# Last pair of row tiles: kept row tiles loaded through ScalarE's queue, last plain tile made by halves of columns in two banks

## The chip, the cores and the metric

The kernel runs on one core of a Trainium2 chip. The metric is the device time of one execution in microseconds (us), the median over runs. The engines are TensorE (PE; PEld is its loading of weights), VectorE (DVE), ScalarE (ACT), GpSimd (POOL) and SyncE (SP, which here only issues DMAs; SPq and ACTq are the queues of instructions that issue them).

## The reference

The output is `x + s * g` for a tensor x of 2048 rows and 448 columns. g is a gated network on the normalised rows; s is the real part of a Fourier transform over the columns and then over the rows, written as matrix products with given matrices:

```python
xn = _layernorm(x, axis=-1)
a = jnp.einsum("bsd,ed->bse", xn, dft_hid_re)
b = jnp.einsum("bsd,ed->bse", xn, dft_hid_im)
s = jnp.einsum("ts,bse->bte", dft_seq_re, a) - jnp.einsum("ts,bse->bte", dft_seq_im, b)
g = silu((gelu(xn @ w_gate) * (xn @ w_up)) @ w_down)
return x + s * g
```

## The kernel before

All matrix products are made from pairs: a number is split in a high part, in the matrix engine's 32-bit format, and a low part, the rest. A product is the sum of high by high, high by low and low by high. `split` makes the high part by a copy on ScalarE and the low part by a subtraction on VectorE.

The work goes in stages: normalised rows are turned and split; the gated network; the transform over columns (the tiles a and b); then the transform over rows, which fills the time from about 477 us on. This last stage alone is touched. It makes the 16 row tiles of the output (128 rows by 448 columns each) in eight pairs j = 0 to 7. A pair takes 16 steps, u0 to u15 in this text. In the steps u0 to u13 (`seven`) one of fourteen row tiles of the transformed input enters seven products of a scheme that needs seven products where eight would be usual; each product has a PSUM bank of its own, and takes a matmul of 448 columns and one of 224. In the last pair the steps u11 to u13 are ordered by product, so that products end one after another. The steps u14 and u15 (`plain`, called t0 and t1) are the two remaining input tiles, 12 matmuls for each of the two output tiles of the pair, in banks of their own (py0, py1). `gather` adds the seven products to the two output tiles c0 and c1 (in `cc`) on VectorE, after a first copy on ScalarE.

Each step needs coefficients: `load_c` loads them on SP's queue (ct and sums for a step of seven, cp for a plain one; in the end x), `sum_c` adds some of them on VectorE (L1208, L1209), and `prep_c` splits them (L149 on ScalarE, L150 on VectorE). In step m, `prep_c` splits for step m + 3, and then loads, into the buffer that came free, for step m + 8. So a late load holds a sum, then a split, and in the end PE.

Of the fourteen row tiles ten lie in SBUF for good. Four, called kept tiles here, share two places (`ts_u`, `ts_g`) and are read back from DRAM (`td`) in every pair, in eight pieces, one in each of u0 to u7 (L1386), on SP's queue. Each piece overwrites the part that PE read last, and waits for PE.

The order of every engine's instructions is that of the code, and an engine waits in order. DMAs of SP and ScalarE take eight semaphores in turn (DMAHW0 to 7): before one is issued, the DMA that used its semaphore last must have landed.

After the last step of the last pair, c1 is multiplied by its gate (`gx`), x is added, c0 gets py0, gate and x and is stored; then the last plain tile is multiplied by the gate, added to c1, and stored, by halves of columns (`sides`), one half on SP's and one on ScalarE's queue.

Of the kernel before, what the change touches and what calls it, by code (L numbers as in the profile page):

```python
# [8 lines left out]
F32 = mybir.dt.float32  # L9
# [4 lines left out]
P = 128  # L14
S = 2048
D = 448
# [28 lines left out]
KP = (10, 15)  # L45
# [14 lines left out]
def fnet_geglu(ctx: ExitStack, tc: tile.TileContext, xw, ca, ct, cp, et, wss, wd, out):  # L60
# [15 lines left out]
    nc = tc.nc  # L76
# [51 lines left out]
    def bank(i, name):  # L128
        return psum.tile([P, 512], F32, name=name, tag=f"b{i}")
# [425 lines left out]
    with tc.manual_schedule():  # L555
# [356 lines left out]
        h, l = [[v[:, n] for n in range(4)] for v in (xth[1], xtl[1])]  # L912
# [74 lines left out]
        for n, (p, f) in enumerate(blocks):  # L987
# [10 lines left out]
            if p == 0:  # L998
# [9 lines left out]
                if f in (8, 11):  # L1008

                    k = slice(0, 4, 3) if f == 8 else slice(1, 3)  # L1010
                    for i in range(2):
                        v, w = [u[:, i * 2048 :][:, :2048] for u in (sp, a_x[1].bitcast(F32))]
                        v, w = [u.rearrange("p (k d) -> p k d", k=4)[:, k] for u in (v, w)]
# [6 lines left out]
            elif f == 3:  # L1020

                late = then(late[0], t1_steps[7][2]), late[1]
                v = sb.tile([P, 8 * D], F32, name="gacc2", tag="u1")
# [3 lines left out]
                v = sb.tile([P, 4096], FR, name="w2", tag="u0")  # L1027
# [76 lines left out]
        TS, ab, behind = {}, {}, []  # L1104
# [108 lines left out]
        def prep_c(m):  # L1213

            if m >= len(units):
                return
            n = (4 if isinstance(units[m][1], str) else 7) * P
            h, l = [v[:, :n] for v in slot_at(m)]
            split(h, l, raw_at(m)[:, :n])
            c_hl[m] = h, l  # L1220
            n = nxt.get(m, m + 5)
            if n:
                load_c(n)
# [91 lines left out]

        sides = slice(0, HD), slice(HD, D)

        def plain(m, py):

            h, l = c_hl.pop(m)  # L1320
            for i, k in enumerate(KP):
                for r in range(2):
                    vh, vl = ab[k][r]
                    o = (2 * i + r) * P
                    a, b = h[:, o : o + P], l[:, o : o + P]
                    final = m == len(units) - 1 and i + r == 2
                    for e in sides if final else [slice(0, D)]:
                        for n, (w, v) in enumerate(((a, vh), (a, vl), (b, vh))):
                            nc.tensor.matmul(  # L1329
                                py[:, e], w, v[:, e], start=i + r + n == 0,  # L1330
                                stop=i + r == 2 and (final or n == 2), skip_group_check=m == len(units) - 1,
                            )

        def gather(ps):

# [29 lines left out]
        for m, (j, k) in enumerate(units):  # L1365
            u = m % UN
            end = j == NK // 2 - 1
            if u == 0:
                ps = {q: bank(banks[i], f"p{q}_{j}") for i, q in enumerate(PRODUCTS)}
            if k in KS:  # L1370
                if not end or u < NS - LAST:
                    seven(m, ps)
                elif u == NS - LAST:

                    seven(m, ps, last_steps)

                at = (0, 1, 2, 3, 4, 5, 6, 7) if j else range(LOAD_AT, LOAD_AT + 8)
                for i in range(8):
                    if u != at[i]:
                        continue  # L1380
                    i, h = divmod(i, 4)
                    TS[KX[(j + 1) % 2][i]] = TS[KX[j % 2][i]]
                    n = KX[(j + 1) % 2][i]
                    a, b = [v.rearrange("p (b d) -> p b d", d=D) for v in (TS[n], td[n])]
                    a, b = a[:, PARTS[h]], b[:, PARTS[h]]
                    nc.sync.dma_start(a.bitcast(F32), b)  # L1386
            else:
                py = bank(banks[7 if k == "t0" else 0], f"py{k[1]}_{j}")
                plain(m, py)
            if end and u in GX_END:  # L1390
                load_gx(j, GX_END.index(u))
            elif u == GX_AT[0]:
                load_gx(j, 0)
            elif u == GX_AT[1] and j:
                load_gx(j - 1, 1)

            if m:
                sum_c(m + 4)
            c0, c1 = cs[0][0], cs[1][0]
            if end and u == NS - LAST:  # L1400
                prep_c(m + 3)
                todo = gather(ps)
                todo.insert(2, lambda: prep_c(m + 4))
                todo.insert(7, lambda: nc.vector.tensor_add(c0, c0, cs[0][1]))
                todo.append(lambda: nc.vector.tensor_add(c1, c1, cs[1][1]))
                for f in todo:
                    f()
            elif end and u > NS - LAST:
                if u == NS:
                    py0 = py  # L1410
                if m < len(units) - 1:
                    continue
                x_ = [raw_at(m + 1 + t)[:, :D] for t in range(2)]
                y = raw_at(m + 3)[:, :D]
                nc.vector.tensor_mul(c1, c1, gx[1])
                nc.vector.tensor_add(c0, c0, py0[:, :D])
                nc.vector.tensor_add(c1, c1, x_[1])
                nc.vector.tensor_mul(c0, c0, gx[0])
                nc.vector.tensor_add(c0, c0, x_[0])
                nc.sync.dma_start(ov[:, NK - 2], c0)  # L1420
                for e in sides:
                    nc.vector.tensor_mul(y[:, e], gx[1][:, e], py[:, e])  # L1422
                for e, eng in zip(sides, (nc.sync, nc.scalar)):
                    nc.vector.tensor_add(c1[:, e], c1[:, e], y[:, e])
                    eng.dma_start(ov[:, NK - 1, e], c1[:, e])
            elif u == NS - 1 and not end:
                todo = gather(ps)
                for f in todo[:3]:
                    f()
                prep_c(m + 3)  # L1430
            elif u == NS and not end:
                for f in todo[3:]:
                    f()
                prep_c(m + 3)
                nc.scalar.activation(kept, py[:, :D], AF.Copy)
            elif u == NS + 1:
                prep_c(m + 3)
                spare = [lambda: nc.vector.tensor_add(c0, c0, kept)]
                spare += give(j, 0)
                spare.append(lambda py=py: nc.vector.tensor_add(c1, c1, py[:, :D]))  # L1440
                spare += give(j, 1)
                banks = banks[1:] + banks[:1]
            else:
                if m:
                    prep_c(m + 3)
                if m == 4:
                    sums14()
                if m == 6:
                    hid_split(14)()
                    load_c(14)  # L1450
                    load_c(15)
                if spare:
                    spare.pop(0)()
                if (u in STORE_AT or end and u == STORE_AT[1] - 1) and stores:
                    stores.pop(0)()
# [66 lines left out]
```

## Time and profile before

| | |
|---|---|
| Time, median of 3 runs | 767.68 us (767.65 to 768.83) |
| Profiled execution: time, span | 768.06 us, 766.3 us |
| PE busy | 760.3 us, 99% |
| PE weight loads busy | 686.6 us, 90% |
| VectorE busy | 637.2 us, 83% |
| ScalarE busy | 351.1 us, 46% |
| GpSimd busy | 120.1 us, 16% |
| Moved by DMA | 162.28 MB, 212 GB/s on average |

The span runs from the first to the last instruction of the profiled execution, 1.76 us less than its time. Busy times overlap between engines. In a timeline row stand start, duration, engine, line, operation and tiles (written <- read), their sizes, and in brackets how long the engine idled before it and what ended that. In a row of a DMA issue the last number is the time from its issue to its landing, in us.

### The profile page before, as it was taken

The page shows a single profiled execution, that of the slowest core. Times are in us where ns is not written, and L with a number is a line of the kernel's source. Part 1 is how long each engine was busy: PE and PEld are TensorE (multiplying, and loading weights), DVE is VectorE, ACT ScalarE, POOL GpSimd, SP SyncE. Part 2 cuts the span into 40 slices and gives each one's busy share as a digit, 9 for nine tenths or more (in the row PEclk, how much of TensorE's full clock was granted, in tenths as well). Part 3 has the DMA queues.
Part 4 walks back from the last instruction along what each step waited for, and adds up shares of the span by engine and source line. Part 5 has one row for each costly group of instructions (what it writes and reads, how often), then busy time and mean ns, then how long its engine had stood idle before and what let it go on. Part 6 is the DMA issues. An engine that isn't in the chain of part 4 may idle for free.

```text
span 766.3 us, 11497 instructions
## 1 busy us (share of the span) xinstructions
PE 760.3 (99%) x4044; PEld 686.6 (90%) x4044; DVE 637.2 (83%) x1088; ACT 351.1 (46%) x499; POOL 120.1 (16%) x162
## 2 busy tenths in 40 slices
PE   9999999999999999999999999999999999999997
PEld 8988888888888888888889999999999999999997
DVE  7987789889989988888975677988889797979786
ACT  5866443443434334343343755544444344444441
POOL 2002231423334223232200000000000000000000
PEclk9999999999999999999999999999999999999999
DMA  8077484849568563728742732869696969888794
GB/s 297 17 222 234 118 251 128 232 157 241 211 128 311 141 207 81 227 79 243 156 181 85 296 165 68 278 224 347 201 354 204 339 220 305 246 280 284 239 321 156
DMA packets 81034, 162.28 MB, mean 212 GB/s; under 512 B 8016, under 2 KB 62800, under 8 KB 79568
## 3 DMA queue, kind: packets, MB, share of 16 engines
q1 hardware_dynamic: 75648, 135.02, 51.6%
q0 software_dynamic: 5184, 26.41, 16.0%
q8 instruction: 32, 0.52, 0.3%
q14 instruction: 26, 0.21, 0.1%
q10 hardware_dynamic: 144, 0.11, 0.0%
HBM read 139.36 MB, written 51.25 MB: 249 GB/s over the span
## 4 chain that ended last, share of the span: by engine, by line
PE 98%; DMA 1%; POOL 0%; DVE 0%; SPq 0%; issue 0%; DVEq 0%
PE x L448 24%; PE p L1303 22%; PE po L422 18%; PE p L1306 10%; PE ab L1119 9%; PE py L1329 5%; PE x L460 4%; PE gu L371 3%; PE gu L596 2%; PE pt L206 1%; DMA raw<-xw 1%; POOL w L277 0%; SPq L156 0%; DVE w L272 0%; DVE f L1422 0%; SPq L260 0%
## 5 line engine op out<-in xcount | busy, mean ns | idle before, releaser
L422 PE MATMUL po<-wd,hs 128*128 128x448 f32 x672 | 146.4, 366 | 0.0
L422 PEld LDWEIGHTS po<-wd,hs 128*128 128x128 f32 x672 | 125.7, 188 | 12.4 <-DVE gacc L435 0.3
L448 PE MATMUL x<-xt,w 128*128 128x512 f32 x432 | 112.1, 390 | 0.0
L448 PEld LDWEIGHTS x<-xt,w 128*128 128x128 f32 x432 | 81.1, 188 | 15.9
L149 ACT ACTIVATE w<-raw 128x896 fp32r<-128x896 f32 (+1 forms) x59 | 53.6, 910 | 62.5 <-DVE raw L1209 21.9
L448 PE MATMUL x<-t,w 128*128 128x512 f32 x276 | 80.2, 390 | 0.0
L1119 PE MATMUL ab<-w,xt 128*128 128x448 f32 x256 | 68.1, 365 | 0.0
L435 DVE TENSOR_TENSOR gacc<-gacc,po 128x448 f32<-128x448 f32 x96 | 58.4, 613 | 5.4 <-PE po L422 5.0
L525 ACT ACTIVATE hs<-tmp 128x512 fp32r<-128x512 f32 x24 | 15.2, 633 | 103.5 <-DVE tmp L523 103.5
L448 PEld LDWEIGHTS x<-t,w 128*128 128x128 f32 x276 | 51.8, 188 | 9.9
L1303 PE MATMUL p<-xt,w 128*128 128x448 f32 x168 | 54.4, 374 | 0.0
L320 POOL TENSOR_TENSOR raw<-raw 128x256 f32<-128x256 f32 x23 | 19.5, 846 | 213.7 <-DMA raw<-wss 187.3
L1355 POOL DMA_DIRECT2D cc<-xw x14 | 12.3, 881 | 252.8 <-DVE raw L1208 96.2
L1119 PEld LDWEIGHTS ab<-w,xt 128*128 128x128 f32 x256 | 48.1, 188 | 3.8
L149 ACT ACTIVATE w<-f 128x896 fp32r<-128x896 f32 (+1 forms) x34 | 30.2, 888 | 40.7 <-DVE f L1209 13.5
L150 DVE TENSOR_TENSOR w<-raw,w 128x896 fp32r<-128x896 f32 (+1 forms) x40 | 41.7, 1045 | 2.0 <-ACT w L149 1.5
L1303 PE MATMUL p<-ts_g,w 128*128 128x448 f32 x112 | 36.4, 374 | 0.0
L1303 PE MATMUL p<-ts_u,ts_tmp 128*128 128x448 f32 x112 | 36.3, 374 | 0.0
L1303 PE MATMUL p<-hs,w 128*128 128x448 f32 x112 | 35.5, 374 | 0.0
L1119 PE MATMUL ab<-wd,xt 128*128 128x448 f32 x96 | 35.1, 365 | 0.0
L339 ACT ACTIVATE w<-raw 128x768 fp32r<-128x768 f32 x24 | 20.3, 845 | 30.3 <-POOL raw L326 30.1
L1303 PEld LDWEIGHTS p<-xt,w 128*128 128x128 f32 x168 | 31.5, 188 | 2.4
(281 smaller groups left out, 1825.8 us busy)
## 6 DMA issues: line engine op xcount, KB each, us to landing
sums<-ca SPq DMA_DIRECT2D x16, 896.0 KB, 8.7
sums<-ca POOLq DMA_DIRECT2D x16, 896.0 KB, 8.9
raw<-ct SPq DMA_DIRECT2D x69, 192.0 KB, 4.1
raw<-wss SPq DMA_DIRECT2D x24, 512.0 KB, 3.7
ts_u<-td SPq DMA_DIRECT2D x24, 448.0 KB, 5.8
ts_g<-td SPq DMA_DIRECT2D x24, 448.0 KB, 6.2
raw<-sums SPq DMA_DIRECT2D x69, 128.0 KB, 4.0
f<-ct SPq DMA_DIRECT2D x39, 192.0 KB, 4.6
```

What stands on the lines that cost most here:

```text
L149: nc.scalar.activation(h, src, AF.Copy)
L150: nc.vector.tensor_sub(l, src, h)
L339: nc.scalar.activation(h[:, :n], src[:, :n], AF.Copy)
L371: nc.tensor.matmul(ps[:, cols], a, xt[:, k, cols], start=n == 0, stop=n == len(mm) - 1)
L422: nc.tensor.matmul(po[:, :D], hs[:, a, kk * P : (kk + 1) * P], wdn[:, b, i], start=n == 0, stop=n == 5,)
L435: nc.vector.tensor_add(ga, ga, po[:, :D])
L448: nc.tensor.matmul(ps, a[i], b[j], start=first and n == 0, stop=n == 2, skip_group_check=True)
L460: nc.tensor.matmul(ps, a[0], x_, start=False, stop=True, skip_group_check=True)
L1119: nc.tensor.matmul(p[:, :D], a, b, start=n == 0, stop=n == len(mm) - 1)
L1303: nc.tensor.matmul(ps[q][:, :D], h, v, start=u % UN == 0, stop=False, skip_group_check=True)
L1306: nc.tensor.matmul(ps[q][:, :HD], l, v[:, :HD], start=False, stop=u % UN == NS - 1, skip_group_check=True,)
L1329: nc.tensor.matmul(py[:, e], w, v[:, e], start=i + r + n == 0, stop=i + r == 2 and (final or n == 2), skip_group_check=m == len(units) - 1,)
```

## The change

Four edits, all for the last pair of output tiles (`end`):

- the eight loads of kept tiles are issued on ScalarE's queue;
- in the last plain step (t1) the 12 matmuls are made for the left 224 columns first, in bank py1, and then for the right 224 in a second bank (py2), where before nine of them took all 448 columns and the last three came as two halves, in one bank;
- the last split (`prep_c(m + 4)` at u11) comes ahead of the copy and the sums of `gather`;
- at the end x is added to c1 before c0 gets py0, and each half of the last tile is multiplied and added before the next one's multiplication.

```diff
-        def plain(m, py):
+        def plain(m, *py):
 
             h, l = c_hl.pop(m)
-            for i, k in enumerate(KP):
-                for r in range(2):
-                    vh, vl = ab[k][r]
-                    o = (2 * i + r) * P
-                    a, b = h[:, o : o + P], l[:, o : o + P]
-                    final = m == len(units) - 1 and i + r == 2
-                    for e in sides if final else [slice(0, D)]:
-                        for n, (w, v) in enumerate(((a, vh), (a, vl), (b, vh))):
-                            nc.tensor.matmul(
-                                py[:, e], w, v[:, e], start=i + r + n == 0,
-                                stop=i + r == 2 and (final or n == 2), skip_group_check=m == len(units) - 1,
-                            )
+            for p, e in zip(py, sides) if len(py) > 1 else [(py[0], slice(0, D))]:
+                n = 0
+                for i, k in enumerate(KP):
+                    for r in range(2):
+                        vh, vl = ab[k][r]
+                        o = (2 * i + r) * P
+                        a, b = h[:, o : o + P], l[:, o : o + P]
+                        for w, v in ((a, vh), (a, vl), (b, vh)):
+                            nc.tensor.matmul(p[:, e], w, v[:, e], start=n == 0, stop=n == 11)
+                            n += 1
...
-                    nc.sync.dma_start(a.bitcast(F32), b)
+                    (nc.scalar if end else nc.sync).dma_start(a.bitcast(F32), b)
             else:
                 py = bank(banks[7 if k == "t0" else 0], f"py{k[1]}_{j}")
-                plain(m, py)
+                both_ = [py, bank(banks[1], "py2")] if m == len(units) - 1 else [py]
+                plain(m, *both_)
...
             if end and u == NS - LAST:
                 prep_c(m + 3)
+                prep_c(m + 4)
                 todo = gather(ps)
-                todo.insert(2, lambda: prep_c(m + 4))
-                todo.insert(7, lambda: nc.vector.tensor_add(c0, c0, cs[0][1]))
+                todo.insert(6, lambda: nc.vector.tensor_add(c0, c0, cs[0][1]))
...
                 nc.vector.tensor_mul(c1, c1, gx[1])
+                nc.vector.tensor_add(c1, c1, x_[1])
                 nc.vector.tensor_add(c0, c0, py0[:, :D])
-                nc.vector.tensor_add(c1, c1, x_[1])
                 nc.vector.tensor_mul(c0, c0, gx[0])
                 nc.vector.tensor_add(c0, c0, x_[0])
                 nc.sync.dma_start(ov[:, NK - 2], c0)
-                for e in sides:
-                    nc.vector.tensor_mul(y[:, e], gx[1][:, e], py[:, e])
-                for e, eng in zip(sides, (nc.sync, nc.scalar)):
+                for p, e, eng in zip(both_, sides, (nc.sync, nc.scalar)):
+                    nc.vector.tensor_mul(y[:, e], gx[1][:, e], p[:, e])
                     nc.vector.tensor_add(c1[:, e], c1[:, e], y[:, e])
                     eng.dma_start(ov[:, NK - 1, e], c1[:, e])
```

ScalarE, steps u4 to u7 of the last pair, with what each instruction waits for. L149 are the splits for the steps u7 to u10 (before, one more, for u11); `ts_g<-td` are pieces of a kept tile. Before:

```order
L149 ACTIVATE w<-f_3559 128x896 [waits DMAHW6_49,DVE_49,DMAHW7_49,PE_49,Activation_49]
L149 ACTIVATE ts_tmp<-f_3559 128x896 [waits DMAHW2_49,DVE_49,DMAHW3_49,PE_49,Activation_49]
L149 ACTIVATE w<-raw 128x896 [waits DMAHW5_49,DVE_49,DMAHW6_49,PE_49,Activation_49]
L149 ACTIVATE w<-raw 128x896 [waits DMAHW0_49,DVE_49,DMAHW1_49,PE_49,Activation_49]
L149 ACTIVATE w<-raw 128x896 [waits DMAHW3_49,DVE_49,DMAHW4_49,PE_49,Activation_49]
```

After:

```order
L1384 DMA ts_g_3513<-td_3364 128x2x448 [waits DMAHW3_49,DMASW5_49]
L149 ACTIVATE w<-f_3559 128x896 [waits DVE_49,DMAHW6_49,PE_49,Activation_49]
L1384 DMA ts_g_3513<-td_3364 128x896 [waits DMAHW6_49]
L149 ACTIVATE ts_tmp<-f_3559 128x896 [waits DVE_49,DMAHW4_49,PE_49,Activation_49]
L1384 DMA ts_g_3513<-td_3364 128x2x448 [waits DMAHW1_49]
L149 ACTIVATE w<-raw 128x896 [waits DVE_49,DMAHW7_49,PE_49,Activation_49]
L1384 DMA ts_g_3513<-td_3364 128x448 [waits DMAHW4_49]
L149 ACTIVATE w<-raw 128x896 [waits DVE_49,DMAHW2_49,PE_49,Activation_49]
```

A piece of a kept tile now stands ahead of each split, and waits for a semaphore of a load that SP issued earlier.

SP, steps u3 to u7: ct and sums load the coefficients of the steps u11, u12 and u13, cp those of u14 and u15. Before:

```order
L1201 DMA raw<-ct 128x384 [waits DMAHW3_49,DVE_49]
L1202 DMA raw<-sums_802 128x256 [waits DMAHW4_49]
L1386 DMA ts_g_3513<-td_3364 128x2x448 [waits DMAHW5_49,PE_49]
L1201 DMA f_3559<-ct 128x384 [waits DMAHW6_49,DVE_49]
L1202 DMA f_3559<-sums_802 128x256 [waits DMAHW7_49]
L1386 DMA ts_g_3513<-td_3364 128x896 [waits DMAHW0_49,PE_49]
L1201 DMA f_3559<-ct 128x384 [waits DMAHW1_49,DVE_49]
L1202 DMA f_3559<-sums_802 128x256 [waits DMAHW2_49]
L1386 DMA ts_g_3513<-td_3364 128x2x448 [waits DMAHW3_49,PE_49]
L1199 DMA raw<-cp 128x512 [waits DMAHW4_49,DVE_49]
```

After:

```order
L1201 DMA raw<-ct 128x384 [waits DMAHW4_49,DVE_49]
L1202 DMA raw<-sums_802 128x256 [waits DMAHW5_49]
L1201 DMA f_3559<-ct 128x384 [waits DMAHW7_49,DVE_49]
L1202 DMA f_3559<-sums_802 128x256 [waits DMAHW0_49]
L1201 DMA f_3559<-ct 128x384 [waits DMAHW3_49,DMAHW2_49,DVE_49]
L1202 DMA f_3559<-sums_802 128x256 [waits DMAHW3_49]
L1199 DMA raw<-cp 128x512 [waits DMAHW6_49,DMAHW5_49,DVE_49]
L1355 DMA out<-cc 128x448 [waits DMAHW6_49,DMASW2_49]
L1199 DMA raw<-cp 128x512 [waits DMAHW7_49,DMAHW1_49,DVE_49]
```

The pieces of kept tiles are gone from between the loads. The loads of u13 (third ct and sums) now wait for the semaphore (3) of the piece that ScalarE issues at u4, the last cp for that (1) of the piece at u6; the piece at u7 waits for the semaphore (4) of the first ct here.

VectorE, from the product of c1 and its gate to the end (f is a spare tile that takes the last plain tile times its gate). Before:

```order
L1415 TENSOR_TENSOR cc<-cc,ts_g_3513 128x448 [waits DMAHW4_49,DVE_49]
L1416 TENSOR_TENSOR cc<-cc,py_7_6709 128x448 [waits PE_49]
L1417 TENSOR_TENSOR cc<-cc,f_3559 128x448 [waits DMAHW2_49,DVE_49]
L1418 TENSOR_TENSOR cc<-cc,ts_g_3703 128x448 [waits DMAHW5_49,DVE_49]
L1419 TENSOR_TENSOR cc<-cc,raw 128x448 [waits DMAHW0_49,DVE_49]
L1422 TENSOR_TENSOR f_3559<-ts_g_3513,py_7_6723 128x224 [waits PE_49]
L1422 TENSOR_TENSOR f_3559<-ts_g_3513,py_7_6723 128x224
L1424 TENSOR_TENSOR cc<-cc,f_3559 128x224 [waits DVE_49] x2
```

After:

```order
L1414 TENSOR_TENSOR cc<-cc,ts_g_3513 128x448 [waits DMAHW4_49,DVE_49]
L1415 TENSOR_TENSOR cc<-cc,f_3559 128x448 [waits DMAHW2_49,DVE_49]
L1416 TENSOR_TENSOR cc<-cc,py_7_6709 128x448 [waits PE_49]
L1417 TENSOR_TENSOR cc<-cc,ts_g_3703 128x448 [waits DMAHW5_49,DVE_49]
L1418 TENSOR_TENSOR cc<-cc,raw 128x448 [waits DMAHW0_49,DVE_49]
L1421 TENSOR_TENSOR f_3559<-ts_g_3513,py_7_6723 128x224 [waits PE_49]
L1422 TENSOR_TENSOR cc<-cc,f_3559 128x224 [waits DVE_49]
L1421 TENSOR_TENSOR f_3559<-ts_g_3513,py_6724 128x224 [waits PE_49]
L1422 TENSOR_TENSOR cc<-cc,f_3559 128x224 [waits DVE_49]
```

Each half of the last plain tile now waits for its own bank, and each sum stands right behind its product.

## The prediction

> **What bounds the kernel now.** I read the page first (span, and the chain that ended last), then the busy time by stretches, the timeline of the last 15 us, and last each late DMA's issue and landing.
>
> ```profile
> span 766.3 us, 11497 instructions
> PE 98%; DMA 1%; POOL 0%; DVE 0%; SPq 0%; issue 0%; DVEq 0%
> ```
>
> The chain is the matrix engine's, 98% of the span. Does anything in the last pair of row tiles, the only place where the change acts, make it wait? The stretches (busy us of each engine, granted clock, DMA share, GB/s):
>
> ```profile
> 686.00:721.50 35.50, 35.50 (x222) 33.74 (x221) 29.79 (x58) 15.43 (x19) 1.75 (x2) 1.00 0.86 274
> 721.50:757.00 35.50, 35.50 (x222) 33.75 (x221) 31.01 (x58) 14.40 (x17) 1.77 (x2) 1.00 0.81 261
> 740.00:750.00 10.00, 10.00 (x66) 9.54 (x65) 6.94 (x14) 3.97 (x5) 0.90 (x1) 1.00 1.07 367
> ```
>
> No: PE is busy for all 35.50 us of the last pair (second row), as in the pair before it, at full clock. ScalarE is busy for 14.40 of them. The DMA engines are full between 740 and 750 (share 1.07, 367 GB/s). So earlier loads can buy nothing on PE; they can only keep a wait from appearing. What can shrink is what follows the last matmul:
>
> ```profile
> 756.78 1.39 PE L1329 MATMUL py<-ts_u,w 128*128 128x448 f32 x6
> 759.22 0.36 PE L1329 MATMUL py<-ts_u,ts_tmp 128*128 128x448 f32 x1
> 761.04 0.60 PE L1329 MATMUL py<-xt,ts_tmp 128*128 128x224 f32 x4
> 761.59 0.28 PE L1329 MATMUL py<-xt,ts_tmp 128*128 128x224 f32 x1
> 755.12 0.62 DVE L1343 TENSOR_TENSOR cc<-cc,p 128x448 f32<-128x448 f32 x1
> 758.69 0.63 DVE L1415 TENSOR_TENSOR cc<-cc,ts_g 128x448 f32<-128x448 f32 x1
> 759.42 0.62 DVE L1416 TENSOR_TENSOR cc<-cc,py 128x448 f32<-128x448 f32 x1
> 759.96 0.62 DVE L1417 TENSOR_TENSOR cc<-cc,f 128x448 f32<-128x448 f32 x1
> 760.50 0.62 DVE L1418 TENSOR_TENSOR cc<-cc,ts_g 128x448 f32<-128x448 f32 x1
> 761.14 0.62 DVE L1419 TENSOR_TENSOR cc<-cc,raw 128x448 f32<-128x448 f32 x1
> 761.90 0.69 DVE L1422 TENSOR_TENSOR f<-ts_g,py 128x224 f32<-128x224 f32 x2
> L1422 DVE TENSOR_TENSOR f<-ts_g,py x2: 380/384/388, 761.9 to 762.2; 128x224 f32<-128x224 f32 x2
> 762.51 0.69 DVE L1424 TENSOR_TENSOR cc<-cc,f 128x224 f32<-128x224 f32 x2
> 763.23 0.37 ACTq L1425 DMA_DIRECT2D out<-cc  x1
> out<-cc ACTq DMA_DIRECT2D x1, 112.0 KB, 1.7
> ```
>
> The last matmul ends at 761.59 + 0.28 = 761.87; VectorE (DVE) starts on the last plain tile at 761.90, ends at 763.20 with its four half-width steps, ScalarE's queue issues the last store at 763.23, it lands 1.7 us later (764.9), and 1.4 us close the span. The steps from 755.12 on come back to back, but for two short waits for PE: L1416 at 759.42 for the first plain tile, L1422 at 761.90 for the second.
>
> **The change, part by part.**
>
> *1. The last plain tile by halves.* It was 9 matmuls of 448 columns and 6 of 224; it becomes 24 of 224. Twelve of 448 take 759.22 - 756.78 = 2.44 us, 0.203 each; five steps of 224 take 761.59 - 761.04 = 0.55 us, 0.11 each. Two halves cost 0.22 where one whole cost 0.203, so nine split ones add 9 x 0.017 = 0.15 us. The first half ends at 759.22 + 11 x 0.11 + 0.28 = 760.71, the second at 759.22 + 23 x 0.11 + 0.28 = 762.03, 0.16 later than now. On the path only if DVE is ready by then.
>
> *2. DVE's last steps.* The add of x to the second tile moves ahead of the add that waits for the first plain tile. Two steps where the second needs the first lie 0.64 apart (760.50, 761.14), two that don't need each other 0.54 (759.42, 759.96). From 758.69: add x 759.33, add plain tile 759.87, multiply 760.51, add x 761.15; so the wait at 759.42 is exchanged for a dependence. Then the halves: multiply half 0 at 761.69 (done on PE since 760.71), add half 0, which needs the step just before: 0.384 + 0.03 = 0.41 later, 762.10; multiply half 1 at 0.30 after that (the distance that 0.69 for two of 0.384 leaves), 762.40, past PE's 762.03; add half 1 at 762.81, end 763.19. Now: 763.20. Half 0 starts 0.21 earlier and two dependences take it back: 0.0 us. Bounds: if PE alone set the end, 762.03 + 0.03 + 2 x 0.39 = 762.84, a gain of 0.36; if all four halves stood 0.41 apart from PE's later end, 762.06 + 3 x 0.41 + 0.38 = 763.67, a loss of 0.47. I take 0.0, because DVE's row of steps is unbroken and of the same count.
>
> *3. The gather.* The last split (tile ts_tmp) moves ahead of the copy of the first product on ScalarE, and its VectorE half ahead of the sums.
>
> ```profile
> 751.96 0.54 ACT L1338 ACTIVATE cc<-p 128x448 f32<-128x448 f32 x1 [0.99 <-PE p L1306]
> 753.80 0.68 DVE L150 TENSOR_TENSOR ts_tmp<-raw,ts_tmp 128x512 fp32r<-128x512 f32 x1
> 745.77 0.45 SPq L1199 DMA_DIRECT2D raw<-cp  x1
> raw<-cp SPq DMA_DIRECT2D x1, 256.0 KB, 6.2
> ```
>
> ScalarE idles 0.99 us before the copy, so a split fits if its data is there; but the load issued at 745.77 landed after 6.2 us, at 751.97. Landing there again, it would hold the copy back by the split's 0.6 us, to 752.6. The sums after it wait for PE again at 755.12 (L1343), and the 0.6 us of L150 are gone from between them, which absorbs it: four steps 0.54 apart from 753.2 reach L1343 at about 754.9. Cost 0; past a landing at about 752.2 each microsecond of lateness is one at the end.
>
> *4. The eight loads of kept tiles go to ScalarE's queue*, one in each of the steps u0 to u7 of the last pair. SP issues eight fewer. On ScalarE each costs an issue, 0.37 us by the store above, so 3.0 us, in steps where it is idle over half the time; behind each the split for three steps ahead is queued.
>
> ```profile
> 726.08 0.36 PE L1303 MATMUL p<-ts_u,ts_tmp 128*128 128x448 f32 x1
> 729.09 0.38 SPq L1386 DMA_DIRECT2D ts_u<-td  x1
> 733.22 0.96 ACT L149 ACTIVATE w<-raw 128x896 fp32r<-128x896 f32 x1 [1.36 <-DVE raw L1209]
> ```
>
> The first (now at 729.09) waits for the first two products of u0, which begins at 726.08; on ScalarE nothing else holds it, so it goes at about 727. A step takes 2.19 us (u10 begins at 748.00: 21.92 / 10). The fifth stands behind the split that ends at 734.18, so at about 735, the seventh two steps later, at about 739.4. Each load also waits until the DMA that last used its semaphore has landed. The worst off is the eighth: it waits for a load that SP issued at 736.16:
>
> ```profile
> 736.16 0.33 SPq L1201 DMA_DIRECT2D raw<-ct  x1
> raw<-ct SPq DMA_DIRECT2D x1, 192.0 KB, 6.7
> 741.57 0.95 ACT L149 ACTIVATE w<-raw 128x896 fp32r<-128x896 f32 x1 [1.20 <-PE p L1303]
> 743.86 1.08 DVE L150 TENSOR_TENSOR w<-raw,w 128x896 fp32r<-128x896 f32 x1
> 748.00 0.38 PE L1303 MATMUL p<-hs,w 128*128 128x448 f32 x1
> ```
>
> 736.16 + 6.7 = 742.9, plus the issue 743.2: the split of step u10 starts there instead of at 741.57, ends at 744.2, its VectorE half at 745.2 instead of 744.9, and PE comes to u10 at 748.00. It costs 0, since 2.8 us of lead remain.
>
> Where the lead is short is step u13:
>
> ```profile
> 740.28 0.33 SPq L1201 DMA_DIRECT2D f<-ct  x1
> f<-ct SPq DMA_DIRECT2D x1, 192.0 KB, 7.7
> 741.30 0.69 SPq L1202 DMA_DIRECT2D f<-sums  x1
> f<-sums SPq DMA_DIRECT2D x1, 128.0 KB, 7.1
> 748.48 0.29 DVE L1208 TENSOR_TENSOR f<-f 128x128 f32<-128x128 f32 x1 [1.43 <-DMA f<-sums]
> 750.25 1.09 DVE L150 TENSOR_TENSOR w<-f,w 128x896 fp32r<-128x896 f32 x1
> 751.66 0.26 PE L1306 MATMUL p<-ts_g,w 128*128 128x224 f32 x1
> ```
>
> Its two loads took 7.7 and 7.1 us; DVE waited 1.43 us for the second, and its low part is ready at 751.34, 0.32 us before PE uses it. With the kept tiles on another queue these loads no longer stand behind them. How fast then? At least as fast as this one, issued at 727.03 before the kept loads began; at worst as slow as now, after a later issue:
>
> ```profile
> raw<-sums SPq DMA_DIRECT2D x1, 128.0 KB, 2.4
> ```
>
> Between 2.4 and 7.1 I take about 5: the bytes stay and the engines are full, but the kept loads, issued from about 727 instead of 729, have their own line. Any value under 7.4 costs and gains nothing, since PE does not wait now.
>
> The Trainium skill ("DMA: Bandwidth & Descriptors", section "Issuing engines are not separate DMA queues") speaks against the load part: all issuers end on the same 16 DMA engines, and a second issuer saves only the issue time. The rows of 2.4 and 7.1 us show how much of a landing is waiting behind others, but no run here shows whether a second queue shortens it. By the rule the u13 loads land as late as now and the sum stays at 0, with 0.32 us to spare; by the rows it is 0 too, with some 2 us to spare. The rule bears only on the chance of a stall.
>
> **Sum.** 0.0 (halves and last steps) + 0 (gather) + 0 (loads) = 0.0 us on the profiled execution's 768.06 (766.3 and 1.76 around it). That execution is 0.38 above the median of 767.68; I put the sum on the median: 767.7 us.
>
> **Rivals.**
> *PE waits at step u13* (slower). The SP load of u13 now waits for a semaphore that the fifth kept load releases. If ScalarE issues that one at about 735 and it takes 7.1 us, as the u13 load does now, SP issues the second u13 load after 742.1, at about 742.5; at 7.1 us it lands at 749.6, 1.2 us later than now: 0.9 us of PE wait, 768.6. If the kept loads, on a line of their own, crowd the load to 8.5 us, it is 2.3 us, 770.0. It decides from a landing at 748.7. For it: full DMA engines, 0.32 us of lead. Against it: the two kept loads that stand among the loads just ahead of it are gone from its queue, and SP issues less.
> *The last load is late* (slower): its issue waits for the seventh kept load. From 739.4 and at 7.1 us that is 746.5, so the last load lands at 752.7, and the gather is 0.5 us past the point in part 3: 768.2. Against it: by then most loads are out.
> *The halves pay* (faster): DVE gets through its steps sooner and PE sets the end, 767.68 - 0.36 = 767.3. For it: half 0 is ready 1.3 us before half 1. Against it: DVE's steps show no gap to give up.
> *The second queue does nothing*: landings as now, 767.7 again.
>
> **How the numbers follow.** The forecast (no term reaches the end) 0.68; the second queue does nothing 0.08; the halves pay 0.08; PE waits at u13 0.12; the last load is late 0.04. A measurement of this kernel can tell about 0.2%, 1.5 us, from no change. Of the rivals only the longer stall at u13 passes that, half of its chance, 0.06; I keep 0.04 more for a stall at several steps and 0.03 for a gain that no row shows. So slower 0.10, same 0.87, faster 0.03. The range: below, the gain of 0.36 and as much again for the median's own spread, 767.1; above, the stall of 0.9 us and the spread to 768.9.
>
> **What would show it.** Right: PE without a gap to the end of the last tile, at about 762.0; L1421 on half 0 at about 761.7, the last store at 763.2; eight kept loads on ScalarE's queue from 727, issues near 0.37 us; the wait of 1.43 us before u13's sum shorter. Wrong: idle time on PE in the last six steps, a split on ScalarE over 2 us behind, the first product's copy later than 752.5, or landings on SP's queue over 7.4 us.

## The result and the profile after

| | before | after |
|---|---|---|
| Median (range), 22 runs each | 767.71 us (767.43 to 768.83) | 769.26 us (768.22 to 770.27) |
| Ratio after to before | | 1.0020, 95% interval 1.0014 to 1.0027 |
| Profiled execution: time, span | 768.06 us, 766.3 us | 768.22 us, 766.3 us |

The kernel became 1.55 us (0.2%) slower. The forecast was no change at 767.7 us, and 769.26 lies outside its range.

The profiled execution of the changed kernel is its quickest of 22. So a second execution of 769.42 us, "after, second profile", stands beside it; it stands for the median better. First the page of the first profile, then one stretch, the last pair, in the first profile and in the second (span, busy us of PE, PEld, DVE, ACT, POOL, granted clock, DMA share, GB/s).

```profile
span 766.3 us, 11508 instructions
PE 94%; DVE 3%; DMA 2%; issue 1%; ACT 1%; ACTq 0%; DVEq 0%
```

```profile
721.50:757.00 35.50, 35.39 (x220) 33.39 (x219) 30.85 (x58) 13.84 (x17) 1.77 (x2) 1.00 0.82 260
```

```profile
721.50:757.00 35.50, 34.55 (x213) 32.33 (x212) 30.49 (x57) 13.93 (x17) 1.77 (x2) 1.00 0.83 263
```

Before, PE was busy for all 35.50 us of this stretch. Now 0.11 us are missing in the first profile and 0.95 in the second, at the same clock (1.00), and the chain of the first has DMA and VectorE in it. The timeline of the second profile names the place: two waits of the weight loads, in brackets, 0.91 + 0.62 = 1.53 us.

```profile
751.36 0.19 PEld L1306 LDWEIGHTS p<-ts_u,xt 128*128 128x128 f32 x1 [0.91 <-DVE xt L150]
752.59 0.19 PEld L1306 LDWEIGHTS p<-ts_g,w 128*128 128x128 f32 x1 [0.62 <-DVE w L150]
```

PE waits for VectorE's low parts of the steps u12 and u13. The chain of waits of the same execution leads back from there (start, duration, what; pieces under 0.1 us left out):

```profile
739.02 9.11 DMA f<-sums
748.16 0.30 DVE f L1208
748.52 0.17 issue
748.69 0.76 DVE xt L150
749.45 0.24 issue
749.69 0.29 DVE f L1208
750.01 0.30 DVE f L1209
750.46 0.96 ACT w L149
751.44 1.10 DVE w L150
752.59 0.37 PE p L1306
```

A load of the sums of u12 takes 9.11 us here, where before it took 6.4 (from 738.89). VectorE idles 1.22 us for it, and then makes the sum for u13 without a wait, as its rows say:

```profile
748.16 0.29 DVE L1208 TENSOR_TENSOR f<-f 128x128 f32<-128x128 f32 x1 [1.22 <-DMA f<-sums]
749.69 0.28 DVE L1208 TENSOR_TENSOR f<-f 128x128 f32<-128x128 f32 x1
```

The low part of u12 stands behind the sum for u13 in VectorE's order, so a late load of either step holds both low parts. The load of u13 lands hardly sooner: in the second profile it was issued at 741.65 and took 7.7 us, to 749.4 (before: 741.30, 7.1 us, 748.4). In this execution u12's load is the one that came last; u13's alone would have held PE about 0.2 us less, by an estimate: its sum starts 0.3 us after the landing, where in e10, which waits for it, it is 0.1.

```profile
741.65 0.43 SPq L1202 DMA_DIRECT2D f<-sums  x1
f<-sums SPq DMA_DIRECT2D x1, 128.0 KB, 7.7
```

A measure for all runs follows from this. *PE late* is the time from the first matmul of u0 to that of t0, less the 30.70 us of before (756.78 - 726.08). It is 0.38 us in the first profile (725.64 to 756.72) and 1.50 in the second (725.61 to 757.81). In the first profile the pair began 0.44 us sooner, in stages that the change does not touch, which is why its span equals that of before.

The end of the kernel, in the first profile:

```profile
759.16 0.82 PE L1329 MATMUL py<-ts_u,ts_tmp 128*128 128x224 f32 x6
759.82 0.83 PE L1329 MATMUL py<-xt,ts_tmp 128*128 128x224 f32 x6
760.49 0.83 PE L1329 MATMUL py<-ts_u,ts_tmp 128*128 128x224 f32 x6
761.16 0.83 PE L1329 MATMUL py<-xt,ts_tmp 128*128 128x224 f32 x6
759.82 0.61 DVE L1416 TENSOR_TENSOR cc<-cc,py 128x448 f32<-128x448 f32 x1
761.67 0.38 DVE L1421 TENSOR_TENSOR f<-ts_g,py 128x224 f32<-128x224 f32 x1
762.08 0.39 DVE L1422 TENSOR_TENSOR cc<-cc,f 128x224 f32<-128x224 f32 x1
762.39 0.38 DVE L1421 TENSOR_TENSOR f<-ts_g,py 128x224 f32<-128x224 f32 x1
762.80 0.39 DVE L1422 TENSOR_TENSOR cc<-cc,f 128x224 f32<-128x224 f32 x1
763.23 0.37 ACTq L1423 DMA_DIRECT2D out<-cc  x1
```

From the start of t0 to VectorE's end it takes 762.80 + 0.39 - 756.72 = 6.47 us (before 6.42). In the second profile 1.50 + 0.06 = 1.56 us are lost in the last pair and behind it, of the 1.71 by which this execution is over before's median: the loss is nearly all PE's wait in the last pair. Some 0.15 us lie outside the span: the time less the span is 1.88 to 2.05 us in the 22 runs of the changed kernel (median 1.94), and 1.72 to 1.92 in the runs of before beside the experiments (median 1.79). Why is not shown.

### The profile page after: what moved, and what is told of

It reads as the page before. It is cut to its first block, busy times and chain, and to the rows that moved or that the text cites. A ratio compares the mean times of both kernels' runs of the same rounds, so it can differ in the third digit from the quotient of the medians.

```text
span 766.3 us, 11508 instructions
## 1 busy us (share of the span) xinstructions
PE 760.5 (99%) x4053; PEld 686.5 (90%) x4053; DVE 636.6 (83%) x1088; ACT 351.9 (46%) x499; POOL 118.7 (15%) x162
## 4 chain that ended last, share of the span: by engine, by line
PE 94%; DVE 3%; DMA 2%; issue 1%; ACT 1%; ACTq 0%; DVEq 0%
PE x L448 24%; PE p L1303 19%; PE po L422 18%; PE ab L1119 9%; PE p L1306 9%; PE x L460 4%; PE py L1329 4%; PE gu L371 3%; PE gu L596 2%; DMA raw<-ct 1%; PE pt L206 1%; PE warm L575 1%; DVE w L150 1%; DMA f<-ct 1%; DVE xt L150 0%
## 5 line engine op out<-in xcount | busy, mean ns | idle before, releaser
L149 ACT ACTIVATE w<-raw 128x896 fp32r<-128x896 f32 (+1 forms) x59 | 53.5, 910 | 65.1 <-DVE raw L1209 20.9
L525 ACT ACTIVATE hs<-tmp 128x512 fp32r<-128x512 f32 x24 | 15.2, 632 | 104.4 <-DVE tmp L523 104.4
L320 POOL TENSOR_TENSOR raw<-raw 128x256 f32<-128x256 f32 x23 | 17.6, 764 | 215.0 <-DMA raw<-wss 131.2
L149 ACT ACTIVATE w<-f 128x896 fp32r<-128x896 f32 (+1 forms) x34 | 30.2, 888 | 38.9 <-PE p L1303 13.5
L1208 DVE TENSOR_TENSOR raw<-raw 128x128 f32<-128x128 f32 x68 | 19.7, 290 | 18.1 <-DMA raw<-sums 18.1
```

Of the source, the lines that this page charges most:

```text
L149: nc.scalar.activation(h, src, AF.Copy)
L1208: eng.tensor_add(s2, cr1, s1)
```

## The experiments

Theories, by the letters that the expectations use. A: the kept loads on ScalarE's queue make PE wait near the end of the pair; A1, since ScalarE waits behind them and its splits come late; A2, since the coefficient loads of u13 on SP's queue come late. B: the halves cost it. C: any second queue does. Later O and S, two accounts of why u13's loads are late. The table has all runs; times from u0 on count from its first matmul, "u13" is its second load (sums), by each run's profile.

| run | u13 issued, landed after u0 (us) | PE late (us) | profiled (us) | median (range) (us) | ratio to before, 95% |
|---|---|---|---|---|---|
| before | 15.2, 22.3 | 0 | 768.06 | 767.71 | |
| after, first profile | 16.9, 22.9 | 0.38 | 768.22 | 769.26 | 1.0014 to 1.0027 |
| e11 after, second profile | 16.0, 23.8 | 1.50 | 769.42 | | |
| e1 queue only | 18.0, 24.0 | 1.86 | 769.86 | 769.40 (768.13 to 770.23) | 1.0011 to 1.0030 |
| e2 halves only | 14.6, 22.4 | 0.00 | 767.68 | 767.87 (767.60 to 768.85) | 0.9994 to 1.0012 |
| e3 GpSimd's queue | 15.7, 19.5 | 0.00 | 768.04 | 767.78 (767.55 to 769.75) | 0.9996 to 1.0013 |
| e4 load behind the split | 17.0, 24.0 | 1.49 | 769.52 | 768.09 (767.95 to 769.52) | 0.9998 to 1.0016 |
| e5 last four loads | 18.1, 24.4 | 1.87 | 769.50 | 769.53 (768.85 to 769.89) | 1.0011 to 1.0029 |
| e6 first four loads | 14.9, 19.9 | 0.00 | 767.62 | 767.77 (767.62 to 768.32) | 0.9991 to 1.0008 |
| e7 ScalarE held | 16.0, 22.5 | 1.15 | 768.85 | 768.92 (768.78 to 769.25) | 1.0006 to 1.0023 |
| e8 add on GpSimd | 17.1, 23.0 | 0.54 | 768.44 | 767.98 (767.65 to 768.44) | 0.9992 to 1.0010 |
| e9 ScalarE held less | 15.7, 20.6 | 0.01 | 767.79 | 768.00 (767.66 to 768.60) | 0.9994 to 1.0012 |
| e10 u13's load held | 17.2, 24.0 | 1.48 | 769.08 | 769.17 (768.98 to 769.74) | 1.0010 to 1.0029 |
| e12 seventh on SP | 14.7, 20.2 | 0.00 | 767.87 | 768.33 (767.87 to 769.14) | 0.9999 to 1.0018 |
| e13 seventh alone | 16.7, 23.4 | 0.97 | 768.99 | 768.77 (768.30 to 769.06) | 1.0003 to 1.0021 |
| e14 as e12, second profile | 14.6, 21.5 | 0.00 | 768.54 | | |
| e15 as e12, third profile | 14.6, 19.7 | 0.00 | 768.64 | | |

Leave e7 out for now. Where u13's second load lands up to 22.4 us after u0, PE is not late; beyond about 22.5 it is late by what is over (22.9: 0.38, 23.0: 0.54, 24.0: 1.48, 24.4: 1.87). Two runs are 0.2 and 0.3 us later than that, e11 and e1: in both the sums of u12 took 9.1 to 9.2 us, and VectorE waited for those and not for u13's.

### Which part of the change: e1, e2, e3

e1 is the kernel before with its eight loads on ScalarE's queue, e2 the changed kernel with them on SP's, e3 with them on GpSimd's:

```diff
-                    (nc.scalar if end else nc.sync).dma_start(a.bitcast(F32), b)
+                    nc.sync.dma_start(a.bitcast(F32), b)                           # e2
+                    (nc.gpsimd if end else nc.sync).dma_start(a.bitcast(F32), b)   # e3
```

> Only the eight loads of kept tiles go to ScalarE's queue; the last plain tile, the gather and the end are as before. Theory A (the loads wait in ScalarE's order and hold the splits behind them): slower by 1.0 to 2.0 us, with a spread over 1 us between executions; the split of u10 starts after 743.5. Theory B (the halves, the second bank and the new order at the end cost the time): within 0.3 us of before. Theory C (a second queue makes the coefficient loads land later): slower by 1 to 2 us as in A, with landings over 7.7 us on SP's queue.

> The changed kernel, but with the eight loads on SP's queue as before. Theories A and C: within 0.3 us of before, with executions as close together as before's. Theory B: slower by 1.0 to 2.0 us.

> The changed kernel, but with the eight loads on GpSimd's queue: still a second queue beside SP's, but no split stands behind them and they take semaphores of another set. Theory A: within 0.3 us of before, ScalarE's split of u10 before 742.5. Theory C: slower by 1 us or more, since the coefficient loads share the DMA engines with a second queue as before. Theory B: slower by 1 to 2 us.

e1 loses as much as the whole change, e2 and e3 can't be told from before. So B falls, and C in its general form too: it is ScalarE's queue. On GpSimd's, u13's second load took only 3.8 us:

```profile
f<-sums SPq DMA_DIRECT2D x1, 128.0 KB, 3.8
```

### Which of the loads: e4, e5, e6

e4 issues each kept load behind the split of its step instead of ahead of it; e5 moves only the last four loads to ScalarE's queue, e6 only the first four:

```diff
+                    if end:                                                        # e4
+                        late_load = lambda a=a, b=b: nc.scalar.dma_start(a.bitcast(F32), b)
...
+                if late_load:
+                    late_load()
...
+                    (nc.scalar if end and i == 1 else nc.sync).dma_start(a.bitcast(F32), b)   # e5
+                    (nc.scalar if end and i == 0 else nc.sync).dma_start(a.bitcast(F32), b)   # e6
```

> The changed kernel, but each of the eight loads is issued on ScalarE's queue behind the split of its step in place of ahead of it. Theory A: the wait is not gone, it stands before the next split; as a load's semaphore was then last used by a load one place later, it is about as long: slower than before by 0.5 to 2.0 us. Theory B: slower by 1 to 2 us, like the changed kernel. Theory C: slower by 1 to 2 us.

> The changed kernel with only the last four loads (u4 to u7) on ScalarE's queue, the first four on SP's as before. Theory A1 (ScalarE held behind its loads is enough: the longest waits, 1.8 and 2.7 us, are those of u6 and u7): slower than before by 0.8 to 2.0 us. Theory A2 (the kept loads that start early on a line of their own, from 726.5, make the coefficient loads land late): the first four start as before, so 0 to 0.7 us.

> The changed kernel with only the first four loads (u0 to u3) on ScalarE's queue, the last four on SP's. Theory A1: the splits of u5 and u6 come about 1 us late and the lead makes it up: 0 to 0.4 us. Theory A2: the early loads are there, the coefficients of u8 to u10 land 2 us later than before: slower by 0.8 to 1.7 us.

The last four make all of the loss, the first four none. e4 loses 0.4 us in the median, which its interval doesn't tell from nothing; the execution that was profiled, its slowest, is late by 1.49 us at u13. Its usual execution is hardly late there: the median span is 766.0 us, that of the runs of before beside it 765.9; the rest of the 0.4 us lies outside the span (time less span 2.12 us against 1.79). It doesn't tell A1 from A2.

### Late splits on ScalarE: e7, e9, and e8 beside them

In the changed kernel the eighth kept load waits until 744.41 for its semaphore, and the splits of u10 and u11 stand behind it. The row looked like the cause (in brackets the idle time of ScalarE):

```profile
744.41 0.33 ACTq L1384 DMA_DIRECT2D ts_g<-td  x1
744.92 1.79 ACT L149 ACTIVATE w<-raw 128x896 fp32r<-128x896 f32 x2 [3.16 <-DMA raw<-ct]
```

e7 and e9 bring that lateness without the queue: the loads stay on SP's, and ScalarE makes copies within a spare tile that nothing reads.

```diff
-                    (nc.scalar if end else nc.sync).dma_start(a.bitcast(F32), b)
+                    nc.sync.dma_start(a.bitcast(F32), b)
+                if end:
+                    for _ in range({2: 5, 3: 5, 5: 3, 6: 6, 7: 9}.get(u, 0)):   # e7; e9: 7: 7
+                        nc.scalar.activation(kept[:, :HD], kept[:, HD:], AF.Copy)
```

> All eight loads on SP's queue as before; ScalarE is held instead by copies of a spare tile ahead of the splits of u5, u6, u8, u9 and u10 (28 copies of 224 columns, whose result nobody reads), so that these splits start about as late as in the changed kernel. Theory A1: slower by 0.8 to 2.0 us. Theory A2: at most 0.4 us, since the loads land as before and the lead of 3 us covers the splits.

> The run with ScalarE held by dummy copies once more, but with seven instead of nine copies ahead of the split of step u10, so that this split starts at about 744.9 as in the changed kernel (745.70 in the first try). The loads of kept tiles stay on SP's queue. Theory A1 (ScalarE's splits come late, and that alone makes PE wait): at least 768.6, PE's first matmul of t0 0.8 us or more late. Theory A2 (the late issue of u13's coefficient loads, behind the semaphore of a kept load, makes most of the loss): within 0.3 us of the halves alone, 767.9, PE without a wait in the last pair, and the 768.9 of the first try is the price of its overshoot of 0.8 us.

In e7 PE was 1.15 us late, which spoke for A1; but its copies held the split of u10 until 745.70, 0.78 us longer than the change does. e9 holds it until the same time as the change, and PE is not late:

```profile
744.92 1.78 ACT L149 ACTIVATE w<-raw 128x896 fp32r<-128x896 f32 x2
745.89 1.09 DVE L150 TENSOR_TENSOR w<-raw,w 128x896 fp32r<-128x896 f32 x1 [2.04 <-ACT w L149]
```

VectorE waits 2.04 us for the split, and that is still in time. A1 falls as the cause: the 3.16 us of ScalarE are within the lead, which e7 overran.

e8 tried a gain at the end: the loads on SP's queue, and x added to c1 by GpSimd instead of VectorE.

```diff
-                nc.vector.tensor_add(c1, c1, x_[1])
+                nc.gpsimd.tensor_add(c1, c1, x_[1])
```

> All eight loads on SP's queue, and in the end the add of x to the last tile on GpSimd in place of VectorE, beside VectorE's steps for the other tile. If VectorE's unbroken row of steps sets the end: faster than the kernel with the halves alone by 0.2 to 0.4 us, the last store at about 0.35 us earlier after the last matmul. If PE or the landing sets it: no change; if GpSimd's add is slower than 2.2 us, later by what it is over.

The add took GpSimd 1.15 us, and VectorE's step beside it 1.15 instead of 0.62, so what VectorE saves it loses again; the time is that of e2 within the measurement. The profiled execution, the slowest of its 11, shows one thing more: u13's second load landed after 23.0 us and PE was 0.54 us late, with all kept loads on SP's queue. So now and then the landing is late with no kept load on ScalarE's queue.

```profile
759.74 1.15 POOL L1415 TENSOR_TENSOR cc<-cc,f 128x448 f32<-128x448 f32 x1 [17.98 <-DVE cc L1414]
760.22 1.15 DVE L1417 TENSOR_TENSOR cc<-cc,ts_g 128x448 f32<-128x448 f32 x1
```

### The late load of u13 by itself: e10, with the second profile e11

e10 keeps the kept loads on SP's queue and leaves ScalarE free; only u13's two coefficient loads are issued one step later.

```diff
-            if n:
+            if n and n != len(units) - 3:
...
+            if n == len(units) - 2:
+                load_c(len(units) - 3)
```

> The changed kernel with the loads of kept tiles on SP's queue, and only the two coefficient loads of step u13 issued one step later, at about 742.5 to 743.5 (740.3 and 741.3 before, 742.2 and 742.6 or later in the changed kernel). ScalarE waits for nothing new. Theory A2 (u13's late load alone): the second of them lands after 749, VectorE's sum waits for it, PE waits 0.8 to 1.5 us at u13, 768.6 to 769.4. Theory A1 (late splits on ScalarE alone): no wait of PE over 0.3 us, at most 768.1.

> The changed kernel as it is, once more, for a profile of an execution nearer its median of 769.26 than the 768.22 of the profiled one. Theory A1 and A2 together: from the first matmul of u0 to the first of t0 32 us or more (30.7 without a wait), with PE waiting for the split of u10 or u11 and for that of u13. If it is 31.1 us again, the loss of the median lies outside the last pair.

This alone costs as much as the change, 769.17 against 769.26 us. Its rows, VectorE first, then the weight loads:

```profile
749.64 0.29 DVE L1208 TENSOR_TENSOR f<-f 128x128 f32<-128x128 f32 x1 [3.18 <-DMA f<-sums]
751.32 0.19 PEld L1308 LDWEIGHTS p<-ts_u,xt 128*128 128x128 f32 x1 [0.89 <-DVE xt L150]
752.54 0.19 PEld L1308 LDWEIGHTS p<-ts_g,w 128*128 128x128 f32 x1 [0.62 <-DVE w L150]
```

VectorE idles 3.18 us for the load, and PE waits at the same two weight loads as in e11, for nearly the same times (0.91 and 0.62 there). A2 is shown: a coefficient load that lands late is enough, with no kept load on ScalarE's queue. In the changed kernel it is u13's alone in the first profile, and u12's with u13's close behind it in the second.

### Why the load is late: e12, e13, and two more profiles of e12

Before, the order of issue at this place was: sixth kept load, u13's two loads, seventh kept load. On ScalarE's queue nothing holds the seventh behind u13's, and in the changed kernel it goes first, at 740.25 (u13's at 742.20 and 742.57). It has 448 KB, at the 335 GB/s that the DMA engines moved here before (734 to 742 us) 1.4 us. Account O: this order makes the loss. Account S: the semaphore of the fifth kept load holds u13's loads. e12 leaves the seventh load on SP's queue and the other seven on ScalarE's, e13 the reverse:

```diff
+                    (nc.scalar if end and u != 6 else nc.sync).dma_start(a.bitcast(F32), b)   # e12
+                    (nc.scalar if end and u == 6 else nc.sync).dma_start(a.bitcast(F32), b)   # e13
```

> The changed kernel, but the kept load of step u6 (the seventh, 448 KB) stays on SP's queue, where it stands behind the coefficient loads of u13, as before the change; the other seven go to ScalarE's queue. Account O (order: on ScalarE's queue the seventh kept load goes out at about 740, ahead of u13's coefficient loads, and its bytes, 448 KB at 335 GB/s or 1.4 us, are moved first): u13's second load lands by 748.3, PE does not wait (at most 0.3 us), at most 768.1. Account S (semaphores: u13's loads are held by the landing of the fifth kept load, which stays as in the changed kernel and now holds the first of the two): issue still after 742.3, PE waits 0.8 us or more, 768.6 to 769.5.

> The changed kernel with all kept loads on SP's queue except that of step u6, which goes to ScalarE's. Account O: it goes out at about 739.5, ahead of u13's loads or with them, and these land 1.0 to 1.5 us later than with all on SP (747.9 there), at about 749: PE waits 0.8 to 1.3 us, 768.7 to 769.3. Account S: u13's loads wait for no kept load on ScalarE's queue, land as with all on SP, and PE does not wait: at most 768.1.

Both came out as O says, but for the time of e12. One kept load of eight on ScalarE's queue costs 1.05 us; the other seven there leave PE in time, with 768.33 us, for which the expectation gave at most 768.1. The rows of e13 (ACTq is the seventh kept load) and of e12:

```profile
739.45 0.40 ACTq L1384 DMA_DIRECT2D ts_g<-td  x1
740.77 0.33 SPq L1201 DMA_DIRECT2D f<-ct  x1
742.67 0.32 SPq L1202 DMA_DIRECT2D f<-sums  x1
```

```profile
739.87 0.33 SPq L1201 DMA_DIRECT2D f<-ct  x1
740.25 1.15 SPq L1202 DMA_DIRECT2D f<-sums  x1
741.49 0.39 SPq L1384 DMA_DIRECT2D ts_g<-td  x1
```

With the seventh load ahead (e13), u13's sums are issued 1.9 us behind its ct, and land 23.4 us after u0; behind u13's loads (e12), they land after 20.2. So the seventh load's place decides. That does not refute semaphores as the means, for e12 moves them too: there the semaphore of the fifth load falls to the seventh load, and not to u13's, as the expectation had it. u13's second load went out at 740.25, before the fifth landed, at 741.08.

A load ahead does two things: it shares the DMA engines, and it takes one turn of the eight semaphores, so u13's loads wait for the semaphores 2 and 3 instead of 1 and 2, which DMAs issued one place later release.

- The semaphores make the later issue. In e13 the load whose semaphore u13's sums take was issued at 736.07 and took 6.6 us, to 742.65; the sums go out at 742.67, 16.7 us after u0. In e2 they take the semaphore of the DMA before that one; it is free at 739.74, and they go out 14.6 us after u0. In the first profile of the changed kernel the two loads are issued at 742.20 and 742.57, just after landings at 742.14 and at 742.54, the latter the fifth kept load's.
- The sharing can be seen too. In e13 the sixth kept load, issued on SP's queue 0.35 us ahead of the seventh, took 9.3 us (7.7 in e2), and u13's ct 8.3 (7.8); its sums took 6.8 (7.8).

The load of 736.07 in e13, its landing, and that of the sixth kept load:

```profile
736.07 0.33 SPq L1201 DMA_DIRECT2D raw<-ct  x1
raw<-ct SPq DMA_DIRECT2D x1, 192.0 KB, 6.6
ts_g<-td SPq DMA_DIRECT2D x1, 448.0 KB, 9.3
```

How the loss divides between the two is not shown: no run moves a semaphore without a load. The place fits three earlier runs: in e5 the seventh load goes out at 742.25, ahead of u13's at 743.27; in e3 GpSimd issues it at 742.90 or later, behind u13's at 741.72; in e6 it is on SP's queue. The first four loads also moved ahead, but of coefficients with more lead. Two profiled executions, the slowest of their runs, are late with the seventh load behind u13's: in e4 it went out at 743.21, and u13's sums at 742.66, held by the semaphore of the fourth kept load, which landed at 742.64; e8 is the other, held by the same semaphore (landed 742.75, issued 742.76). So the seventh load's place makes most of the loss, but it is not the only way to a late landing.

The profiled execution of e12 was its quickest, so there are two more profiles, for the 0.6 us over before that its median has left:

> The kernel with only the seventh kept load on SP's queue, once more, for a profile of an execution nearer its median of 768.33 than the 767.87 of the profiled one. If the loss of 0.6 us that is left comes from u13's coefficient loads, still held by the semaphore of the fifth kept load, they are issued after 742 and the second lands more than 22.5 us after the start of u0, with PE late by the excess. If not, PE is on time at t0 and the rest lies elsewhere.

> The kernel with only the seventh kept load on SP's queue, a third execution of it, with the same two outcomes: PE late at t0 by as much as the second load of u13 lands later than 22.5 us after the start of u0, or PE on time there and the rest of 0.6 us elsewhere.

They took 768.54 and 768.64 us; u13's second load was issued 14.6 us after u0 in both and landed after 21.5 and 19.7, and PE was not late (726.11 to 756.81 and 726.27 to 756.97, 30.70 each). So this rest is not a wait in the last pair. The interval, 0.9999 to 1.0018, doesn't exclude that there is none, but half of it can be placed: it lies outside the span. The time less the span is 2.05 to 2.24 us in the 11 runs of e12, and 1.72 to 1.91 in those of before beside it, medians 2.10 and 1.79. The span itself is 0.3 us longer (766.2 against 765.9). Why either is so stays open.

## Why the prediction was wrong

**What bounds the kernel** held: PE's chain, with u13's coefficients as a place with little lead. That u12's could come last too it did not say.

**Part 1, the halves,** was right: halves at 0.11 us a matmul, PE's end at 761.16 + 0.83 = 761.99 (forecast 762.03).

**Part 2, VectorE's last steps,** was right to 0.02 us in the first profile: 761.67, 762.08, 762.39, 762.80 (forecast 761.69, 762.10, 762.40, 762.81), the store at 763.23 (763.2). Part of that is luck, for the row began 0.07 us sooner than forecast (758.62, 758.69). "The halves pay" did not come: e2 alone moved nothing.

**Part 3, the gather,** was right: in the first profile the first product's copy starts at 751.91, before the 752.5 named as too late. In the second it starts at 753.00, since PE is late.

**Part 4, the loads, failed**: the term for u13's loads, put at 0, is the step that was wrong. It was made of two values, and both came out worse. The first is the landing, "Between 2.4 and 7.1 I take about 5": the loads took 6.0 and 5.9 us in the first profile and 7.6 and 7.7 in the second. The 2.4 us came from a load issued at 727.03, in a stretch where the DMA engines were not full (share 0.73 from 726 to 734 us), and said nothing of a full one. The second is the issue: "any value under 7.4 costs nothing" counts from the issue of before, 741.30, 15.2 us after u0; it became 742.57 and 741.65, 16.9 and 16.0 us after u0. In the first profile 5.9 us from the old issue would have cost nothing; it is the later issue that makes PE wait. Nor were the kept loads gone from ahead of u13's. The working put the seventh kept load at 739.4 and knew u13's issue at 740.28, but never set the two side by side: one kept load *more* now stood ahead. And u12's loads, of which the prediction says nothing, took 9.1 us in the second profile and held VectorE longest.

**The rival "PE waits at step u13"** is what happened. It gave the issue at about 742.5 (first profile 742.57), a decision from a landing at 748.7, which is 22.6 us after u0 (measured about 22.5), and 768.6 to 770.0 us (769.26). Its chance of 0.12 was too low because of the 5 us above. Its reason, the semaphore of the fifth kept load, is what holds the second load in the first profile (734.77 + 7.8 = 742.6); in the second that semaphore is free at 740.58, and the one that u13's ct takes holds both (landed 741.22, ct issued 741.28). e12 and e13 show that the seventh load's place settles which semaphores u13's loads wait for.

**The eighth kept load** was mis-sized without harm: split of u10 at 744.92, not 743.2, since the load whose semaphore the eighth takes took 8.1 us, not 6.7. The lead of 2.8 us that the prediction gave from 743.2 covered it, as e9 shows. So the sign "a split over 2 us behind" was a bad one: the split was over 3 us behind, and it was not the cause.

**The rule of the Trainium skill** ("DMA: Bandwidth & Descriptors", section "Issuing engines are not separate DMA queues"), that DMAs of all issuers interleave on the same 16 engines, agrees with e13: the sixth kept load, on SP's queue, took 9.3 us with the seventh behind it on ScalarE's, and 7.7 in e2. What it would have told here was drawn too weakly: "land as late as now" holds only if the common order and the turn of the semaphores stay as they were.

## What to carry to other kernels

With the DMA engines full, as here (share 0.98 to 1.06 from 734 to 742 us), a second queue moved no more (291 to 345 GB/s, against 335 to 349 with the kept loads on SP's); it changed the order of the transfers, and which load waits for which semaphore. So before moving a transfer to another queue, write the issues of all queues in one list by time, before and after, and look which urgent load gets one more ahead of it, and whose landing its semaphore then waits for. A long wait on a row (3.16 us on ScalarE here) is a suspect, not a cause: bring the same lateness about by other means, and as exactly as possible, for 0.8 us too much of it (e7) gave the wrong answer.

## What was not expected of the hardware

In the stretch from 734 to 742 us the DMA engines moved less where ScalarE's queue issued seven or all eight kept loads. The rows of before, of e11 and of e10, in this order:

```profile
734.00:742.00 8.00, 8.00 (x53) 7.63 (x52) 7.86 (x17) 3.48 (x5) 1.68 (x2) 1.00 1.05 335
```

```profile
734.00:742.00 8.00, 8.00 (x53) 7.65 (x52) 7.77 (x17) 3.66 (x4) 1.25 (x2) 1.00 1.04 303
```

```profile
734.00:742.00 8.00, 8.00 (x53) 7.65 (x52) 7.68 (x16) 3.79 (x4) 1.77 (x2) 1.00 1.05 349
```

At a DMA share of 1.04 to 1.05 that is 303 GB/s against 335 and 349. Over all profiles it is 291 to 328 GB/s with seven or eight kept loads on ScalarE's queue (shares 0.98 to 1.04), and 335 to 349 with at most four there or all on another (shares 1.04 to 1.06). In e11 more had been moved by then: 299 GB/s from 726 to 734 us, against 223 before. Single landings reached 9.3 us, in e13. Why the rate fell was not tried.
